# Transposing normalised activations with the DMA crossbar instead of TensorE, PSUM and ScalarE, in a four-layer kernel on one core

## The chip, the cores and the metric

The kernel runs on one core of a Trainium2 chip. The metric is the device time of one execution in microseconds (us), as the median over runs; one execution of each kernel was also profiled. A ratio is the mean time of one kernel's fast runs over the mean of the other's in the same rounds, so it is not quite the ratio of the medians quoted beside it.

## The reference, cut to what matters

One sequence of 2048 tokens with 576 features passes through four residual layers: attention-like, gated MLP, attention-like, gated MLP. The same weights serve both pairs.

```python
x = x + _A_ref(_layernorm(x), A_wqkv, A_w_phi, A_wo)     # "A": linear attention, 32 heads of 18
x = x + _B_ref(_layernorm(x), B_w_gate, B_w_up, B_w_down) # "B": (g * u) @ w_down, inner width 4608
x = x + _A_ref(_layernorm(x), ...)
x = x + _B_ref(_layernorm(x), ...)
```

Every layer needs the normalised x with features on the partitions (`xT`), while the normalisation itself works with tokens on the partitions. So each of the 16 tiles of 128 tokens is transposed once per layer, 64 times in all. Layer A first sums over all tokens; only after this barrier can its output be computed. A "pass" below is the part of layer A from its first projection to the barrier.

Of the kernel before, what the change touches and what calls it, by code (L numbers as in the profile page):

```python
# [6 lines left out]
BF16 = mybir.dt.bfloat16  # L7
F32 = mybir.dt.float32
ALU = mybir.AluOpType
# [423 lines left out]
def d_act(n, psum=False, ptrs=0):  # L433
    return n / 1.2 + (63.0 if psum else 92.0) + 93.0 * ptrs
# [10 lines left out]
class K:  # L445
    def __init__(self, nc, A_x, A_wqkv, A_w_phi, A_wo, B_w_gate, B_w_up, B_w_down, out, nlayers=4, dump=None):
        self.nc = nc
        self.A_x, self.A_wqkv, self.A_w_phi, self.A_wo = A_x, A_wqkv, A_w_phi, A_wo
        self.wg, self.wu, self.wd, self.out = B_w_gate, B_w_up, B_w_down, out
        self.nlayers = nlayers  # L450
        self.dump = dump
        self.nln0 = 3
        self.early = 2
        self.NPS, self.NSM, self.NVX, self.NET, self.NXP, self.NWD = 2, 4, 2, 3, 3, 3
        self.sbuf_check = True
        self.lag = 2
        self.bias = {10: 300.0}
        self.qfuse_after = ("ain", 1, 1)
        self.rawq_early = False
        self.v_early = False  # L460
        self.tr = Tracker()
        self.sc = Sched(self.tr)
        self.stack = ExitStack()

    def alloc(self):
        nc = self.nc
        A = lambda name, shape, dt: self.stack.enter_context(nc.sbuf_tensor(name, shape, dt))
        self.ident = A("ident", [128, 128], BF16)
        self.onesf = A("onesf", [128, 128], F32)
        self.epst = A("epst", [128, 1], F32)  # L470
        self.mask = A("mask", [TW, TW], BF16)
        self.ind = A("ind", [TW, HT], BF16)
        self.BDphi = A("BDphi", [TW, NT, TW], BF16)
        self.BD = A("BD", [TW, 2 * NT, 114], BF16)
        self.x_sb = A("x_sb", [128, NS, D], BF16)
        self.xT = A("xT", [128, 6, S], BF16)
        self.Wq = A("Wq", [128, 4, D], BF16)
        self.Wqr = A("Wqr", [128, 288], BF16)
        self.Wk = A("Wk", [128, 4, D], BF16)
        self.Wkr = A("Wkr", [128, 288], BF16)  # L480
        self.Wv = A("Wv", [128, 4, DP], BF16)
        self.Wvr = A("Wvr", [128, 324], BF16)
        self.Wo = A("Wo", [128, 4, D], BF16)
        self.Wor = A("Wor", [128, 288], BF16)
        self.Wg = A("Wg", [128, 4, FF], BF16)
        self.Wu = A("Wu", [128, 4, FF], BF16)
        self.Wr = A("Wr", [128, FF], BF16)
        AT = lambda name, shape, dt, base: nc.alloc_sbuf_tensor_at(name, shape, dt, offset=base)
        self.NG, self.NH = 3, 4
        al32 = lambda n: (n + 31) // 32 * 32  # L490
        raw_b = al32(5 * (2 * D + 72) * 2)
        wt_b = 2 * NT * 128 * 2
        wd_b = al32(self.NWD * CH * D * 2)
        ring_b = (self.NG + self.NH) * 256 * 2
        n1 = max(raw_b + wt_b, wd_b + ring_b)
        arena1 = A("arena1", [128, n1 // 2], BF16)
        a1 = nc.lookup_mloc(arena1).addr
        self.Wraw = AT("Wraw", [128, 5, 2 * D + 72], BF16, a1)
        self.WT = AT("WT", [TW, 2, NT, 128], BF16, a1 + raw_b)
        self.wdr = AT("wdr", [128, self.NWD, CH, D], BF16, a1)  # L500
        self.gsb = AT("gsb", [128, self.NG, 256], BF16, a1 + wd_b)
        self.hT = AT("hT", [128, self.NH, 256], BF16, a1 + wd_b + self.NG * 512)
        self.xln = A("xln", [128, 2 * self.NXP, 640], BF16)
        self.st = A("st", [128, 2 * self.NXP, 12], F32)
        self.mv = A("mv", [128, 2 * self.NXP, 2], F32)
        self.lnv = A("lnv", [128, 2 * self.NXP], F32)
        self.rstd = A("rstd", [128, 2 * self.NXP], F32)
        self.nmean = A("nmean", [128, 2 * self.NXP], F32)
        self.psb = A("psb", [128, self.NPS, D], BF16)
        self.mxmn = A("mxmn", [128, self.NPS, 2, H], F32)  # L510
        self.dd = A("dd", [128, self.NSM, 2, DP], BF16)
        self.ss = A("ss", [128, self.NSM, 2 * H], F32)
        self.rr = A("rr", [128, self.NSM, 2 * H], F32)
        self.wst = A("wst", [TW, NT, DH], BF16)
        self.vx = A("vx", [128, self.NVX, NT, TW + 1], BF16)
        self.eT = A("eT", [TW, self.NET, 2 * NT, 128], BF16)
        self.den = A("den", [128, self.NET, NT * HT], F32)
        self.rden = A("rden", [128, self.NET, NT * HT], F32)
        self.o = A("o", [128, self.NET, DP], BF16)
        self.oT = A("oT", [128, self.NET, 6, 128], BF16)  # L520
        self.ps = self.stack.enter_context(nc.psum_tensor("ps", [128, 8, 512], F32))
        self.psb16 = [self.ps[:, i, :].bitcast(BF16) for i in range(8)]
        self.sbuf_left = nc.sbuf_bytes_remaining
        sc = self.sc
        sc.pool("xlnp", self.NXP)
        sc.pool("sm", self.NSM)
        sc.pool("psb", self.NPS)
        self.vx_of = {}
        self.wt_of = {}
        sc.pool("vx", self.NVX)  # L530
        sc.pool("et", self.NET)
        sc.pool("wt", 2)
        sc.pool("wd", self.NWD)
        sc.pool("pb", 3)
        sc.pool("pbx", 2)
        self.banks = {"pb": [5, 6, 7], "pbx": [3, 4]}
        self.KV_BANKS = [0, 1, 2]
        self.GU_BANKS = [0, 1]
        self.ACC0 = 2
        self.wd_slot = {}  # L540
        self.g_wd = [self.tr.dma_group("wd%d" % i) for i in range(self.NWD)]
# [10 lines left out]
    def t_init(self):  # L552
        s = self
        yield ("ops", "dve", [
            Op(100, lambda e: e.memset(s.epst[:], EPS), writes=[("epst",)]),
            Op(100, lambda e: e.memset(s.wst[:, NT - 1, :], 0.0), writes=[("wst",)]),
            Op(300, lambda e: e.memset(s.xln[:, :, 576:640], 0.0), writes=[("xlnpad",)]),
        ])
        yield ("sig", "wstz")
        yield ("ops", "pool", [  # L560
# [5 lines left out]
               reads=[("onesf",)], writes=[("ident",)]),  # L566
# [3 lines left out]
               reads=[("onesf",)], writes=[("mask", 0)]),  # L570
# [3 lines left out]
               reads=[("onesf",)], writes=[("ind", 0)]),  # L574
# [5 lines left out]
               reads=[("mask", 0)], writes=[("mask", 0), ("mask",)]),  # L580
# [3 lines left out]
               reads=[("ind", 0)], writes=[("ind", 0), ("ind",)]),  # L584
# [3 lines left out]
        yield ("ops", "act", [  # L588
            Op(1000, lambda e: e.memzero(s.Wraw[64:128, 4, 0:2 * D]), writes=[("Wraw", 1)]),
            Op(300, lambda e: e.memzero(s.Wraw[:, :, 2 * D:2 * D + 72]), writes=[("Wraw", 2)]),  # L590
            Op(1800, lambda e: e.memzero(s.xT[0:64, 5, :]), writes=[("xTz",)]),
            Op(300, lambda e: e.memzero(s.Wv[:, :, D:DP]), writes=[("Wvpad",)]),
            Op(100, lambda e: e.memzero(s.Wvr[64:128, 252:324]), writes=[("Wvrpad",)]),
            Op(300, lambda e: e.memzero(s.oT[0:64, :, 5, :]), writes=[("oTz",)]),
# [147 lines left out]
    def t_ln(self, b, sig):  # L742
        s = self
        x_sb, xln, st, mv, lnv, rstd, xT = s.x_sb, s.xln, s.st, s.mv, s.lnv, s.rstd, s.xT
# [3 lines left out]
        ops = []  # L748
# [22 lines left out]
        for j in range(2):  # L771
            ops.append(Op(800, (lambda e, j=j: e.tensor_scalar(  # L772
                xln[:, sl[j], 0:576], x_sb[:, ss[j], :], nm[:, sl[j]:sl[j] + 1], rstd[:, sl[j]:sl[j] + 1],
                ALU.add, ALU.mult)),
                reads=[("x", ss[j], 0), ("x", ss[j], 1), ("nmean", pair), ("rstd", pair), ("xlnpad",)], writes=[("xln", sl[j])]))
        yield ("ops", "pool", ops)
        for j in range(2):
            got = yield ("acq", ["pb", "pbx"])
            bank = s.bank_of(got)
            pT = s.psb16[bank]  # L780
            ops = []
            for k in range(5):
                ops.append(Op(60, (lambda e, j=j, k=k, pT=pT: e.transpose(pT[:, 128 * k:128 * k + 128], xln[:, sl[j], 128 * k:128 * k + 128], s.ident[:])),  # L783
                              reads=[("xln", sl[j]), ("ident",)], writes=[("pbd", bank)], excl=[("pb", bank)]))
            yield ("ops", "pe", ops)
            tok = slice(128 * ss[j], 128 * ss[j] + 128)
            yield ("ops", "act", [
                Op(d_act(640, True), (lambda e, pT=pT, tok=tok: e.copy(xT[:, 0:5, tok], pT[:, 0:640].rearrange("p (k n) -> p k n", k=5))),
                   reads=[("pbd", bank)], writes=[("xT", ss[j], 0)], excl=[("pb", bank)]),
                Op(258, (lambda e, pT=pT, tok=tok: e.copy(xT[64:128, 5, tok], pT[0:64, 512:640])),  # L790
                   reads=[("pbd", bank), ("xTz",)], writes=[("xT", ss[j], 1)], excl=[("pb", bank)]),
            ])
            yield ("rel", got[0], got[1])
        yield ("rel", "xlnp", pair)
        yield ("sig", sig)

# [469 lines left out]
```

## The kernel before: what the change and the argument touch

The kernel writes one fixed instruction list per engine. Python generators describe the work of a tile, a list scheduler with its own time estimates decides in which order the pieces go onto each engine, and a tracker adds the semaphore waits. What matters here is that **every engine runs its list in order**, SyncE too, which issues all DMAs.

```python
self.nln0 = 3                 # pairs of tiles whose normalisation is launched at the start
self.NXP = 3                  # (in one line with others) buffers for a pair of normalised tiles
self.qfuse_after = ("ain", 1, 1)   # after which tile the q weights are prepared
```

The end of the normalisation of a pair of tiles:

```python
# GpSimd: xln = (x - mean) * rstd, 128 x 576
for j in range(2):
    got = yield ("acq", ["pb", "pbx"]); ...                     # a PSUM bank
    for k in range(5):                                          # TensorE, five 128x128 transposes
        Op(60, e.transpose(pT[:, 128*k:128*k+128], xln[:, sl[j], 128*k:128*k+128], s.ident[:]))
    Op(..., e.copy(xT[:, 0:5, tok], pT[:, 0:640]...))           # ScalarE, PSUM -> SBUF
    Op(258, e.copy(xT[64:128, 5, tok], pT[0:64, 512:640]))      # ScalarE, last 64 features once more
```

The loads, all on SyncE's queue, none of them waiting for anything:

```python
yield from xload(0); ...  # x, w_phi, k weights, v weights, rest of x, q weights, output weights
...
yield from grp("wgu", items, "wloaded")     # the MLP's gate and up weights, 10.6 MB, ten DMAs
```

The down weights are streamed in each MLP stage through three buffers (`wdr`), a chunk of 432 KB for three steps of the loop.

## Time and profile before

| | before |
|---|---|
| median | 1252.32 us (1251.99 to 1252.72) |
| first projection of the first pass | 19.7 us |
| first barrier | 97.5 us |
| first MLP stage | 125.1 to 641.2 us |
| second barrier | 703.2 us |
| second MLP stage | 732.2 to 1247.7 us |

The times of the stages are read from the start of the first projection, of the first barrier product and of the first gate matmul, and from the end of the last residual addition of each MLP stage. In the MLP stages TensorE is full; in the first pass VectorE is the fullest engine (71 of 77.5 us), with TensorE, ScalarE and GpSimd close behind (65 to 66 us). The lines for this stand in the prediction.

### The profile page before, as it was taken

The numbers are of one execution on the slowest core, as the hardware profiler recorded it, in microseconds if no ns is written. First come the engines' busy times: TensorE is split into PE (matmuls) and PEld (weight loads), VectorE is DVE, ScalarE is ACT, GpSimd is POOL, SyncE is SP. The second block draws the span as 40 slices with busy tenths as digits, with TensorE's granted clock in tenths as the row PEclk, the third lists the DMA queues.
The fourth block names the chain that finished last, engine by engine and source line by source line (L and its number), as shares of the span: only waits on it lengthen the run. The fifth ranks groups of instructions, "written<-read, shape, count | busy, mean of one in ns | idle before, by whom it ended". The sixth has DMA issues, their size and how long they took to land.

```text
span 1250.4 us, 25739 instructions
## 1 busy us (share of the span) xinstructions
PE 1198.8 (96%) x11096; PEld 936.1 (75%) x11096; DVE 619.3 (50%) x1478; ACT 546.4 (44%) x1393; POOL 272.5 (22%) x268
## 2 busy tenths in 40 slices
PE   6796999999999999999999889999999999999998
PEld 4574777778787777777767568778777777777776
DVE  6898646445553323323269974455445332323232
ACT  7887545445353323222258765444444322222222
POOL 4796212112120000000039742112112000000000
PEclk9998999999999999999999889999999999999999
DMA  9700122222222333333320002222222233323232
GB/s 316 230 2 1 41 75 72 74 85 72 85 73 86 88 99 89 98 90 97 94 64 2 1 2 73 86 82 74 82 84 82 86 97 99 105 91 110 87 109 67
DMA packets 85832, 104.61 MB, mean 84 GB/s; under 512 B 4374, under 2 KB 84566, under 8 KB 84566
## 3 DMA queue, kind: packets, MB, share of 16 engines
q1 hardware_dynamic: 85718, 102.96, 27.0%
q8 instruction: 87, 1.43, 0.5%
q14 instruction: 27, 0.22, 0.1%
HBM read 100.59 MB, written 2.36 MB: 82 GB/s over the span
## 4 chain that ended last, share of the span: by engine, by line
PE 84%; DVE 6%; POOL 5%; ACT 4%; issue 0%; DMA 0%; SPq 0%; DVEq 0%
PE ps L1071 25%; PE ps L1076 25%; PE ps L1109 20%; PE ps L808 4%; PE ps L1019 3%; POOL dd L869 3%; PE ps L1112 3%; DVE ss L855 2%; PE ps L946 2%; POOL dd L833 1%; PE ps L965 1%; PE ps L783 1%; DVE dd L841 1%; PE ps L998 1%; DVE mxmn L823 1%; DVE mxmn L828 1%
## 5 line engine op out<-in xcount | busy, mean ns | idle before, releaser
L1086 DVE TENSOR_TENSOR hT<-ps,gsb 128x256 bf16<-128x256 f32 x576 | 243.9, 423 | 577.2 <-ACT gsb L1084 575.9
L1084 ACT CAST gsb<-ps 128x256 bf16<-128x256 f32 x576 | 214.2, 372 | 621.7 <-PE ps L1076 585.3
L1109 PE MATMUL ps<-wdr,hT 128*128 128x512 bf16 x1152 | 357.5, 379 | 0.4 <-DVE x_sb L1135 0.4
L1071 PE MATMUL ps<-xT,Wg 128*128 128x256 bf16 x2304 | 347.2, 273 | 0.0
L1076 PE MATMUL ps<-xT,Wu 128*128 128x256 bf16 x2304 | 346.1, 273 | 0.0
L1071 PEld LDWEIGHTS ps<-xT,Wg 128*128 128x128 bf16 x2304 | 187.2, 98 | 80.8
L1076 PEld LDWEIGHTS ps<-xT,Wu 128*128 128x128 bf16 x2304 | 225.7, 98 | 26.4
L1112 PE MATMUL ps<-wdr,hT 128*128 128x64 bf16 x1152 | 221.9, 193 | 0.5 <-DVE x_sb L1138 0.5
L869 POOL TENSOR_TENSOR dd<-dd,rr 128x576 bf16<-128x576 bf16 x128 | 146.1, 1163 | 121.1 <-ACT rr L863 121.1
L1109 PEld LDWEIGHTS ps<-wdr,hT 128*128 128x128 bf16 x1152 | 112.6, 98 | 76.8 <-DVE x_sb L1135 0.7
L1071 PE MATMUL ps<-xT,Wr 128*128 128x256 bf16 x576 | 157.2, 273 | 0.0
L1076 PE MATMUL ps<-xT,Wr 128*128 128x256 bf16 x576 | 157.2, 273 | 0.0
L772 POOL TENSOR_SCALAR xln<-x_sb,nmean,rstd 128x576 bf16<-128x576 bf16 x64 | 51.9, 821 | 367.1 <-ACT rstd L767 366.9
L833 POOL TENSOR_TENSOR dd<-psb,mxmn 128x576 bf16<-128x576 bf16 x64 | 74.4, 1163 | 231.6 <-DVE mxmn L823 231.6
L1112 PEld LDWEIGHTS ps<-wdr,hT 128*128 128x128 bf16 x1152 | 112.7, 98 | 6.5 <-DVE x_sb L1138 0.8
L855 DVE TENSOR_REDUCE ss<-dd 128x64 f32<-128x1152 bf16 x64 | 86.4, 1350 | 22.8 <-ACT dd L850 22.5
L1071 PEld LDWEIGHTS ps<-xT,Wr 128*128 128x128 bf16 x576 | 56.5, 98 | 6.6
L1076 PEld LDWEIGHTS ps<-xT,Wr 128*128 128x128 bf16 x576 | 56.4, 98 | 6.6
L820 ACT CAST psb<-ps 128x288 bf16<-128x288 f32 x128 | 47.9, 400 | 17.3 <-PE ps L808 15.3
L949 ACT COPY eT<-ps 108x768 bf16<-108x768 bf16 x64 | 50.8, 798 | 8.5 <-PE ps L965 4.9
L828 DVE TENSOR_REDUCE mxmn<-ps 128x16 f32<-128x288 f32 x128 | 52.0, 448 | 0.0
L841 DVE TENSOR_TENSOR dd<-ps,mxmn 128x288 bf16<-128x288 f32 x128 | 51.7, 447 | 0.0
(85 smaller groups left out, 1143.8 us busy)
## 6 DMA issues: line engine op xcount, KB each, us to landing
wdr<-in_B_w_down_dram SPq DMA_DIRECT2D x192, 432.0 KB, 3.3
Wg<-in_B_w_gate_dram SPq DMA_DIRECT2D x4, 1152.0 KB, 12.3
Wu<-in_B_w_up_dram SPq DMA_DIRECT2D x4, 1152.0 KB, 27.3
x_sb<-in_A_x_dram SPq DMA_DIRECT2D x4, 576.0 KB, 5.8
out_dram<-x_sb SPq DMA_DIRECT2D x8, 288.0 KB, 3.7
Wraw<-in_A_wqkv_dram SPq DMA_DIRECT2D x8, 144.0 KB, 4.8
Wv<-in_A_wqkv_dram SPq DMA_DIRECT2D x1, 576.0 KB, 3.9
Wo<-in_A_wo_dram SPq DMA_DIRECT2D x1, 576.0 KB, 6.6
```

The lines of the kernel that those rows point to most:

```text
L772: ops.append(Op(800, (lambda e, j=j: e.tensor_scalar(xln[:, sl[j], 0:576], x_sb[:, ss[j], :], nm[:, sl[j]:sl[j] + 1], rstd[:, sl[j]:sl[j] ...
L828: ops.append(Op(370, (lambda e, h=h, pv=pv: e.tensor_reduce(mxmn[:, pz, 1, 16 * h:16 * h + 16], pv, AX.X, ALU.min)), reads=[("pbd", bank)] ...
L833: yield ("ops", "pool", [Op(1170, (lambda e: e.tensor_tensor(d1, p3, mxb, ALU.subtract)), reads=[("psb", pz, 0), ("psb", pz, 1), ("mx", pz ...
L841: ops.append(Op(370, (lambda e, d2h=d2h, pv=pv, mnbh=mnbh: e.tensor_tensor(d2h, pv, mnbh, ALU.subtract)), reads=[("pbd", bank), ("mn", pz, ...
L855: Op(1320, (lambda e: e.tensor_reduce(ss[:, sm, :].rearrange("p (b g) -> p b g", b=2), e4, AX.X, ALU.add)), reads=s.ddk(sm, 0) + s.ddk(sm, ...
L869: yield ("ops", "pool", [Op(1150, (lambda e, ev=ev, rb=rb: e.tensor_tensor(ev, ev, rb, ALU.mult)), reads=s.ddk(sm, br) + [("rr", sm), ("dd ...
L1071: ops.append(Op(d_pe(256), (lambda e, lhsT=lhsT, rhs=rhs, k=k, gub=gub: e.matmul(ps[:, gub, 0:256], lhsT, rhs, start=(k == 0), stop=(k == ...
L1076: ops.append(Op(d_pe(256), (lambda e, lhsT=lhsT, rhs=rhs, k=k, gub=gub: e.matmul(ps[:, gub, 256:512], lhsT, rhs, start=(k == 0), stop=(k = ...
L1084: yield ("ops", "act", [Op(372, (lambda e, g=g, gub=gub: e.copy(gsb[:, g, :], ps[:, gub, 0:256])), reads=[("GUg", gub)], writes=[("gsb", g ...
L1086: yield ("ops", "dve", [Op(425, (lambda e, g=g, h=h, gub=gub: e.tensor_tensor(hT[:, h, :], ps[:, gub, 256:512], gsb[:, g, :], ALU.mult)), ...
L1109: ops.append(Op(d_pe(512), (lambda e, lhsT=lhsT, bank=bank, slot=slot, fi=fi, f2=f2: e.matmul(ps[:, bank, 0:512], lhsT, s.wdr[:, slot, fi, ...
L1112: ops.append(Op(d_pe(64) + 6, (lambda e, lhsT=lhsT, sl=sl, slot=slot, fi=fi, f2=f2: e.matmul(ps[:, Z, 64 * sl:64 * sl + 64], lhsT, s.wdr[: ...
```

## The change

The intent is to take work from TensorE, which is full for most of the program, and from ScalarE and PSUM. The crossbar transpose is a DMA from SBUF to SBUF. It needs a 128 x 768 source with the last 64 features twice, so GpSimd writes a second small piece; the wider buffers leave room for two pairs only.

```diff
-        self.nln0 = 3
+        self.nln0 = 2
-        ... self.NXP, self.NWD = 2, 4, 2, 3, 3, 3
+        ... self.NXP, self.NWD = 2, 4, 2, 3, 2, 3
+        self.g_xt = [self.tr.dma_group("xt%d" % i) for i in range(2 * self.NXP)]
-        self.xln = A("xln", [128, 2 * self.NXP, 640], BF16)
+        self.xln = A("xln", [128, 2 * self.NXP, 768], BF16)
-            Op(1800, lambda e: e.memzero(s.xT[0:64, 5, :]), writes=[("xTz",)]),
+            ops.append(Op(200, (lambda e, j=j: e.tensor_scalar(
+                xln[:, sl[j], 704:768], x_sb[:, ss[j], 512:576], ...     # GpSimd, 128x64
-            (acquire a bank, five e.transpose on TensorE, two e.copy on ScalarE, release)
+            yield ("dma", s.g_xt[sl[j]], (lambda e, j=j, tok=tok: e.dma_start_transpose(xT[:, :, tok], xln[:, sl[j], :])), ...)
```

More of the change, by code (lines that the diff above doesn't have):

```diff
@@ L451, in __init__ @@
         self.dump = dump
-        self.nln0 = 3
+        self.nln0 = 2
         self.early = 2
-        self.NPS, self.NSM, self.NVX, self.NET, self.NXP, self.NWD = 2, 4, 2, 3, 3, 3
+        self.NPS, self.NSM, self.NVX, self.NET, self.NXP, self.NWD = 2, 4, 2, 3, 2, 3
         self.sbuf_check = True
@@ L556, in t_init @@
             Op(100, lambda e: e.memset(s.wst[:, NT - 1, :], 0.0), writes=[("wst",)]),
-            Op(300, lambda e: e.memset(s.xln[:, :, 576:640], 0.0), writes=[("xlnpad",)]),
+            Op(300, lambda e: e.memset(s.xln[:, :, 576:704], 0.0), writes=[("xlnpad",)]),
         ])
@@ L775, in t_ln @@
                 reads=[("x", ss[j], 0), ("x", ss[j], 1), ("nmean", pair), ("rstd", pair), ("xlnpad",)], writes=[("xln", sl[j])]))
+            ops.append(Op(200, (lambda e, j=j: e.tensor_scalar(
+                xln[:, sl[j], 704:768], x_sb[:, ss[j], 512:576], nm[:, sl[j]:sl[j] + 1], rstd[:, sl[j]:sl[j] + 1],
+                ALU.add, ALU.mult)),
+                reads=[("x", ss[j], 0), ("x", ss[j], 1), ("nmean", pair), ("rstd", pair), ("xlnpad",)], writes=[("xln", sl[j], 1)]))
         yield ("ops", "pool", ops)
         for j in range(2):
-            got = yield ("acq", ["pb", "pbx"])
-            bank = s.bank_of(got)
-            pT = s.psb16[bank]
-            ops = []
-            for k in range(5):
-                ops.append(Op(60, (lambda e, j=j, k=k, pT=pT: e.transpose(pT[:, 128 * k:128 * k + 128], xln[:, sl[j], 128 * k:128 * k + 128], s.ident[:])),
-                              reads=[("xln", sl[j]), ("ident",)], writes=[("pbd", bank)], excl=[("pb", bank)]))
-            yield ("ops", "pe", ops)
-            tok = slice(128 * ss[j], 128 * ss[j] + 128)
-            yield ("ops", "act", [
-                Op(d_act(640, True), (lambda e, pT=pT, tok=tok: e.copy(xT[:, 0:5, tok], pT[:, 0:640].rearrange("p (k n) -> p k n", k=5))),
-                   reads=[("pbd", bank)], writes=[("xT", ss[j], 0)], excl=[("pb", bank)]),
-                Op(258, (lambda e, pT=pT, tok=tok: e.copy(xT[64:128, 5, tok], pT[0:64, 512:640])),
-                   reads=[("pbd", bank), ("xTz",)], writes=[("xT", ss[j], 1)], excl=[("pb", bank)]),
-            ])
-            yield ("rel", got[0], got[1])
+            tok = slice(128 * ss[j], 128 * ss[j] + 128)
+            yield ("dma", s.g_xt[sl[j]], (lambda e, j=j, tok=tok: e.dma_start_transpose(xT[:, :, tok], xln[:, sl[j], :])),
+                   [("xln", sl[j]), ("xln", sl[j], 1)], [("xT", ss[j], 0), ("xT", ss[j], 1)], 128 * 768 * 2, False, True)
         yield ("rel", "xlnp", pair)
```

## The prediction

> **What bounds the kernel now.** I read the slice table first, to see where one engine is full and where none is.
>
> ```profile
> PE   6796999999999999999999889999999999999998
> DVE  6898646445553323323269974455445332323232
> POOL 4796212112120000000039742112112000000000
> DMA  9700122222222333333320002222222233323232
> ```
>
> Each digit is 31 us. There are four stages, two of each kind. In slices 0 to 3 and 20 to 23 (the attention-like halves) TensorE is not full and VectorE or GpSimd is. In slices 4 to 19 and 24 to 39 (the gated MLP halves, with the tail of the attention output mixed in) TensorE is full and little else matters. The DMA engines are full only in slices 0 and 1, when all weights are loaded.
>
> Second, the stretch table, which puts microseconds to this. Columns: busy time (count) of PE, weight load, VectorE, ScalarE, GpSimd, then granted clock, DMA share, GB/s.
>
> ```profile
> 20.00:97.50 77.50, 66.18 (x647) 48.72 (x646) 71.10 (x143) 66.37 (x179) 64.59 (x60) 1.00 0.44 152
> 125.00:160.00 35.00, 33.41 (x337) 26.77 (x336) 22.93 (x56) 20.81 (x50) 11.47 (x11) 0.99 0.13 40
> 160.00:400.00 240.00, 240.00 (x2299) 191.45 (x2298) 120.43 (x310) 108.31 (x274) 42.09 (x42) 1.00 0.26 78
> 400.00:640.00 240.00, 240.00 (x2145) 186.86 (x2143) 75.64 (x191) 64.37 (x178) 6.49 (x8) 1.00 0.32 94
> 747.00:1000.00 253.00, 251.81 (x2410) 200.47 (x2408) 125.46 (x317) 112.47 (x279) 44.65 (x43) 1.00 0.27 80
> ```
>
> From 20 to 97.5 us VectorE is busy 71.1 of 77.5 us: the first attention pass is VectorE-bound and can hardly be squeezed. From 160 to 640 us TensorE is busy in every microsecond, so each TensorE instruction taken out there shortens the program by its own length.
>
> Third, the same stretches for the TensorE transposes alone (PE, weight load, clock, DMA).
>
> ```profile
> 20.00:97.50 77.50, 4.12 (x50) 3.17 (x50) 1.00 0.44 152
> 125.00:160.00 35.00, 0.89 (x10) 0.73 (x10) 0.99 0.13 40
> 160.00:400.00 240.00, 7.99 (x90) 6.38 (x90) 1.00 0.26 78
> 400.00:640.00 240.00, 3.54 (x40) 2.91 (x40) 1.00 0.32 94
> 747.00:1000.00 253.00, 6.19 (x70) 5.09 (x70) 1.00 0.27 80
> ```
>
> Fourth, the start, in the timeline: when the first transposes and projections run, and what the SyncE queue is issuing then.
>
> ```profile
> 10.12 0.71 PE L783 MATMUL ps<-ident,xln 128*128 128x128 bf16 x5 [1.27 <-POOL xln L772]
> ...
> 15.00 2.21 SPq L670 DMA_DIRECT2D Wg<-in_B_w_gate_dram  x4
> ...
> 18.40 2.02 SPq L674 DMA_DIRECT2D Wu<-in_B_w_up_dram  x4
> ...
> 19.76 0.70 PE L808 MATMUL ps<-Wk,xT 128*128 128x288 bf16 x4
> ```
>
> The first token tile is transposed at 10.1 us and the first projection starts at 19.8 us, while SyncE is queueing the MLP weights up to 20.4 us. Those weights arrive much later; the view of the tile Wu and the page's list of DMA issues show it:
>
> ```profile
> DMA to landing us min/median/max: 23.8/27.3/30.8
> ```
>
> ```profile
> Wg<-in_B_w_gate_dram SPq DMA_DIRECT2D x4, 1152.0 KB, 12.3
> Wu<-in_B_w_up_dram SPq DMA_DIRECT2D x4, 1152.0 KB, 27.3
> ```
>
> The last Wu piece is issued at about 20.0 us and lands 30.8 us later, at 50.8 us. Today nothing on the early path waits for it.
>
> **What the Trainium skill says.** (1) "DMA: Bandwidth & Descriptors", section "Queues, rings and completion order": a queue has one ring on each DMA engine, and descriptors on an engine are consumed in ring order. The trace agrees: on the one queue the landing time grows in issue order, 12.3 us for Wg, 27.3 us for Wu. (2) The same page, "Latency and other measured facts", gives the DMA transpose 261 GB/s in one kernel; "Advanced Engine Details and Errata", section "X-Bar Transpose (TRN2)", says 350 to 400 GB/s. No run here shows it yet. (3) "VectorE: DVE Perf Modes", section "The three transpose paths": a 128x128 bf16 transpose is 390 ns on TensorE and 1309 ns by the crossbar. The trace has 219 ns for one on TensorE, and because they are pipelined, 0.089 us each in the stream (7.99 us / 90).
>
> **The change part by part.**
>
> Removed from TensorE: 64 token tiles x 5 = 320 transposes. Only those in TensorE-bound stretches count: 0.89 + 7.99 + 3.54 = 12.4 us in 125 to 640 us, and 6.2 us in 747 to 1000 us. Sum 18.6 us gained. The 4.1 us in the first pass lie beside a full VectorE and count little.
>
> Removed from ScalarE: 64 evictions of 128x640 (692 ns) and 64 of 64x128 (257 ns), together 61 us, and one clearing of xT (1.04 us). ScalarE bounds no long stage; I count 2 to 3 us in the first pass, where it is 86% busy beside VectorE, and nothing elsewhere.
>
> Added to GpSimd: 64 copies of 128x64. The 128x576 one costs 821 ns; in proportion the small one is 91 ns, and with some fixed cost I estimate 0.2 us. Sixteen of them are in the first pass: 3 us on an engine busy 64.6 of 77.5 us. I count 1 us.
>
> Added to the DMA: 64 transposes of 128 x 768 x 2 B = 196,608 B. The wdr loads (442,368 B) land 3.3 us after issue; at the 330 GB/s that the weight load reaches in 20 to 40 us, 1.3 us of this is data, so about 2 us is fixed. With 261 GB/s for the transpose (0.75 us) I estimate 2.7 us, say 3 us, from issue to landing. The unfavourable reading, six 128-column blocks at 1.31 us one after another, is 7.9 us; I give that little weight, since it counts the fixed part six times.
>
> Moved: the transposes now go through SyncE, an in-order engine with one queue. The scheduler gives every weight load to SyncE before the first transpose, because the loads wait for nothing. **This is the main term.** The first transposes can be issued after 20.4 us at the earliest, and in ring order they stand behind all the MLP weights. They move when those have landed, at 50.8 us; the first xT tile is there at about 52 us and the first projection starts at about 52.5 instead of 19.8 us: 32.7 us late. What can be done in the hole? Little: the q weights are fused only after a processed tile, and with two xln pairs only the statistics of four pairs of tiles run ahead, which they did before too. From there the first pass needs its VectorE time of 71 us plus a few us to start, 75 instead of 77.8 us. So the barrier comes at about 127.5 instead of 97.5 us: +30 us.
>
> Start of each MLP stage: before, the second xln tile of the first pair is ready at 122.3 us and the gate matmuls start 3.1 us later (125.4). Now two small GpSimd copies (0.4 us) and a transpose of some 3 us stand there. About +1 us each, +2 us for both. Later pairs have a whole block (36 steps of 1.58 us, 57 us) of slack. Pairs for the second attention pass are normalised one MLP block at a time and are hidden as well; only the last pair, ready at 647 us, could matter, and there TensorE no longer stands waiting for xln (3.7 us of waits). I count 0.
>
> Weight stream of the MLP: one wdr chunk is used in 3 x 1.58 = 4.7 us, three buffers, so a load has 9.5 us less 3.3 us of landing: about 6 us of slack. A pair of transposes ahead of it on the queue costs about that, or less if they overlap. I count +2 us in all.
>
> Sum: 1252.3 + 30 + 1 + 2 + 2 - 18.6 = 1268.7; the ScalarE relief is already inside the 75 us. I round to 1268 us.
>
> **The rivals.**
>
> A: the transposes do not wait behind the weights. Then the 30 us are gone and the change is 18.6 us gained less some 5 us: about 1239 us, within 2%. Against it: the rising landing times. For it: no trace here has a crossbar transpose, and it might be served apart. I give it 1 in 9.
>
> B: the transpose is slow, 5 to 8 us, and does not overlap with its neighbour. Then in the first pass sixteen of them need 80 to 128 us against VectorE's 71 us, and the barrier comes up to 50 us later still; and a pair would take 10 to 16 us of the wdr loads' 6 us of slack, so TensorE would stall in many blocks. That makes 1290 to 1400 us. For it: 1309 ns for one 128x128 block. Against it: both bandwidth figures. I give it 1 in 5.
>
> C: the TensorE gain is not collected, because SyncE stands in order, with a transpose waiting for xln holding up a wdr load that is ready. Its time would be about 1280 us. Against it: the three buffers, and that the scheduler places both by their ready times.
>
> D: the gain is all there is and the late start is absorbed by the stages after. Against it: the barrier needs all sixteen tiles, and TensorE is full from 160 us on, so nothing later can absorb it.
>
> **Range and chances.** The main case spreads by the late start (27 to 34 us) and the MLP hiccups (0 to 10 us): 1260 to 1280. Rival A pulls the lower end down, B the upper end up: 1245 to 1295. Faster by 2% needs less than 1227.8 us, more than even A gives: 0.02. Slower by 2% needs over 1277.3 us: B, C and the upper edge of the main case: 0.30. The rest, 0.68.
>
> **What would show each step.** The late start: the first projection at 50 to 55 us and TensorE nearly idle between 22 and 50 us; if it is at 25 us, rival A. The transposes' size: landing 2.5 to 4 us after issue in quiet stages, 25 us or more for the first four. The TensorE gain: PE busy time down by about 24 us in all and each MLP stage shorter by 12 and 6 us from its first to its last matmul. Rival B or C: waits of TensorE for wdr in the MLP stages, which are absent today. A landing time near 8 us, or a barrier much later than 130 us, would make the prediction wrong on the slow side.

## The result

The changed kernel takes 1280.68 us (median of 4 runs, 1279.59 to 1282.26) against 1252.15 us; the ratio is 1.0229, interval 1.0214 to 1.0243. It is slower by just over 2%, and correct.

By stage, from both traces (us):

| stage | before | after | difference |
|---|---|---|---|
| start to first projection | 19.7 | 52.0 | +32.3 |
| first pass, to the barrier | 77.8 | 86.5 | +8.7 |
| barrier to first gate matmul | 27.6 | 28.1 | +0.5 |
| first MLP stage | 516.1 | 510.9 | -5.2 |
| second pass, to its barrier | 62.0 | 61.9 | -0.1 |
| barrier to gate matmul | 29.0 | 28.5 | -0.5 |
| second MLP stage | 515.5 | 506.9 | -8.6 |
| sum | 1247.7 | 1274.8 | +27.1 |

All of the loss is before the first barrier (41.0 us); the stages after it give 13.9 us back. The slice table of the changed kernel's page shows the hole:

```profile
PE   1388689999999999999999969999999999999998
DVE  3297865554645333232328986555554332323232
POOL 2287641221311000000006963222121000000000
DMA  9812013333323343443321002333233433333332
```

In the first two slices (64 us) TensorE, VectorE and GpSimd are busy for only one to three tenths of the time, while the DMA engines are full. The SyncE rows of the changed kernel's timeline from 13 to 60 us, and the TensorE rows from 50 to 58 us, say what was awaited:

```profile
18.16 2.01 SPq L674 DMA_DIRECT2D Wu<-in_B_w_up_dram  x4
20.21 39.17 SPq L783 DMA_TRANSPOSE xT<-xln  x8
```

```profile
51.97 1.14 PE L799 MATMUL ps<-Wk,xT 128*128 128x288 bf16 x4 [38.76 <-DMA xT<-xln]
...
56.86 0.65 PE L799 MATMUL ps<-Wk,xT 128*128 128x288 bf16 x4
```

The first transpose is issued right behind the last weight load, and the 38.76 us for which TensorE sat idle before its first projection end when it lands. The two rows also show that the first matmuls after the hole run at about half pace: four take 1.14 us at 52 us and 0.65 us at 57 us.

The view of the transposing line, the page's list of DMA issues, and the view of the added GpSimd line (nanoseconds: minimum, median, maximum):

```profile
DMA to landing us min/median/max: 2.5/2.6/31.7
```

```profile
xT<-xln SPq DMA_TRANSPOSE x64, 2.6
```

```profile
L776 POOL TENSOR_SCALAR xln<-x_sb,nmean,rstd x64: 390/393/398, 10.0 to 1003.6; 128x64 bf16<-128x64 bf16 x64
```

A transpose of 196,608 B lands in 2.6 us where nothing stands in its way. The small GpSimd copy takes 0.39 us, half as long as one of nine times the width.

The stretches of the changed kernel that answer to those of before, with the same columns:

```profile
52.00:138.50 86.50, 67.57 (x591) 47.58 (x592) 70.98 (x142) 56.89 (x153) 69.83 (x74) 0.95 0.22 48
200.00:440.00 240.00, 236.83 (x2206) 189.47 (x2244) 124.12 (x317) 96.32 (x246) 52.17 (x63) 1.00 0.34 94
440.00:677.00 237.00, 235.06 (x2060) 184.03 (x2095) 75.94 (x192) 57.35 (x162) 9.45 (x16) 1.00 0.37 97
```

In the first pass no engine is busy for more than 71 of 86.5 us, where before VectorE was busy for 71 of 77.8 us. In the MLP stages TensorE seems to have small gaps, but this trace lacks 162 of the 1152 matmuls of one line (990 are recorded), so I do not read them as idle time; the lengths of the blocks, below, are the sounder measure.

### The profile page after: what moved, and what is told of

Same layout as the page of the kernel before. It is cut to its first block, busy times and chain, and to the rows that moved or that the text cites. A ratio compares the mean times of both kernels' runs of the same rounds, so it can differ in the third digit from the quotient of the medians.

```text
span 1277.9 us, 24939 instructions
## 1 busy us (share of the span) xinstructions
PE 1172.5 (92%) x10614; PEld 919.1 (72%) x10776; DVE 618.4 (48%) x1478; ACT 490.1 (38%) x1264; POOL 295.7 (23%) x332
## 4 chain that ended last, share of the span: by engine, by line
PE 82%; POOL 7%; DVE 3%; DMA 3%; ACT 2%; SPq 1%; issue 1%; DVEq 0%
PE ps L1062 25%; PE ps L1067 24%; PE ps L1100 17%; PE ps L1103 5%; PE ps L799 5%; POOL dd L860 4%; PE ps L1010 3%; DMA xT<-xln 3%; POOL dd L824 2%; PE ps L937 2%; PE ps L956 1%; DVE ss L846 1%; PE ps L989 1%; POOL xln L772 1%; ACT eT L940 0%
## 5 line engine op out<-in xcount | busy, mean ns | idle before, releaser
L1100 PE MATMUL ps<-wdr,hT 128*128 128x512 bf16 x990 | 318.1, 380 | 0.4 <-DVE x_sb L1126 0.4
L772 POOL TENSOR_SCALAR xln<-x_sb,nmean,rstd 128x576 bf16<-128x576 bf16 x64 | 52.5, 820 | 403.2 <-ACT rstd L767 365.1
L799 PE MATMUL ps<-Wk,xT 128*128 128x288 bf16 x256 | 41.9, 291 | 42.0 <-DMA xT<-xln 38.8
L814 DVE TENSOR_REDUCE mxmn<-psb 128x32 f32<-128x576 bf16 x64 | 47.7, 746 | 44.1 <-ACT psb L811 44.0
L799 PEld LDWEIGHTS ps<-Wk,xT 128*128 128x128 bf16 x256 | 24.7, 99 | 50.9 <-DMA xT<-xln 38.9
```

Of the source, the lines that this page charges most:

```text
L772: ops.append(Op(800, (lambda e, j=j: e.tensor_scalar(xln[:, sl[j], 0:576], x_sb[:, ss[j], :], nm[:, sl[j]:sl[j] + 1], rstd[:, sl[j]:sl[j] ...
L799: ops.append(Op(d_pe(ncol), (lambda e, lhsT=lhsT, rhs=rhs, k=k: e.matmul(s.ps[:, bank, 0:ncol], lhsT, rhs, start=(k == 0), stop=(k == 4))) ...
L1100: ops.append(Op(d_pe(512), (lambda e, lhsT=lhsT, bank=bank, slot=slot, fi=fi, f2=f2: e.matmul(ps[:, bank, 0:512], lhsT, s.wdr[:, slot, fi, ...
```

## The experiments

Three questions were open: is it the order in the queue that makes the start late; why is the first pass 8.7 us longer; and what did the MLP stages gain per transpose, with what hidden costs. All kernels gave correct results.

### weights_act: the MLP weights on another queue

```diff
+        yield ("wait", ("xT", 1, 1))                     # after the first two pairs are normalised
-        yield from grp("wgu", items, "wloaded")
+        yield from grp("wgu", items, "wloaded", "act")   # ScalarE issues these ten DMAs
```

(Here and in own_ring the scheduler keeps a DMA estimate for each queue, so it also lays out another order of instructions.)

> The changed kernel, but the ten MLP weight loads are issued from ScalarE's DMA queue, after the first two pairs of tiles are normalised; the transposes stay on SyncE's queue. Theory (the transposes wait behind the weights because they share a ring): the first transposes land within some 3 to 8 us of their issue, the first projection starts at 20 to 26 us instead of 52 us, and the time falls by about 28 us to 1250 to 1256 us. Rival (it is the load on the DMA engines, or the crossbar is held up by any large load, whatever the queue): the first projection stays at about 50 us and the time at about 1280 us.

Measured: 1286.7 us, ratio 1.0282 (1.0226 to 1.0338), and the first projection at 59.3 us, later than in the changed kernel. So moving the weights away from the transposes' ring did not help at all. The test was not clean: the q weights and the output weights still stood before the transposes on SyncE's queue, and the output weights landed 28.5 us after issue (37.3 us for their small remainder, in two pieces) instead of 6.7 us. The next run cleans this.

### own_ring: nothing before the transposes on their queue

```diff
-        (q weights and output weights on SyncE's queue before the MLP weights)
+        (output weights, MLP weights, q weights, in this order, all on ScalarE's queue)
```

> The changed kernel, but ScalarE's DMA queue issues the MLP weights, the output projection's weights and the q weights, in this order; so on SyncE's queue nothing but the finished early loads stands before the first transposes, and both queues are active from about 12 us. Ring order as the cause: the first transposes land within 15 us of their issue, first projection before 30 us. Rival (two rings share the engines unfairly, or a crossbar transpose is held up by loads on the engines whatever the ring): first projection at 45 us or later, as in the run with only the MLP weights moved (59 us), where two small loads still stood before the transposes.

Measured: 1297.49 us (two runs, 1291.7 and 1303.28; the time itself is of little use, since the q weights now come last). First projection at 25.5 us. But it is one tile only; the TensorE rows of this kernel's timeline, 24 to 30 and 40 to 50 us:

```profile
25.46 1.14 PE L801 MATMUL ps<-Wk,xT 128*128 128x288 bf16 x4 [12.48 <-DMA xT<-xln]
```

```profile
44.40 1.14 PE L801 MATMUL ps<-Wk,xT 128*128 128x288 bf16 x4 [16.20 <-DMA xT<-xln]
```

and the landing times of the first 150 us, followed by the stretch from 20 to 50 us in this kernel and in the changed one (columns as before; the last is GB/s):

```profile
DMA to landing us min/median/max: 2.5/3.2/53.6
```

```profile
20.00:50.00 30.00, 6.51 (x25) 3.43 (x25) 0.00 (x0) 0.00 (x0) 0.00 (x0) 0.53 1.05 243
20.00:50.00 30.00, 0.00 (x0) 0.00 (x0) 0.00 (x0) 0.00 (x0) 0.00 (x0) 0.50 1.02 345
```

The first two transposes, issued at 10.7 and 12.5 us, land at 25.4 and 44.4 us, while the last MLP weights land at 70 us. This alone proves little, since both were issued before the first MLP weight load (13.5 us). The trace's records of single DMA packets decide it. In the changed kernel no 256 B piece of a transpose starts before 49.1 us, when the weights run out (their last piece starts at 50.4 us), so on the shared queue **ring order is the cause**. With a ring of their own the transposes move all the time, but slowly. The counts from 30 to 60 us in own_ring (q1 is SyncE's queue, q10 ScalarE's; packets, MB, share of the engines):

```profile
q10 hardware_dynamic: 1071, 7.38, 94.3%
q1 hardware_dynamic: 1074, 0.27, 8.5%
```

The two queues take turns packet by packet, and not byte by byte: 1074 packets of some 250 B against 1071 of some 6.9 KB. A transpose consists of 800 packets (the changed page counts 51,200 more for 64 transposes), so about as many weight packets pass beside it. My estimate from these numbers, 800 x 7.1 KB at 256 GB/s, is 22 us for each transpose; the first three land 19 and 25 us apart (25.4, 44.4 and 69.5 us), and one took 53.6 us from issue to landing. So the rival was right too: beside a full load a crossbar transpose is slow even with a ring to itself. Either of the two is enough to make the first pass late. The load is slowed as well: from 20 to 50 us the DMA engines move 243 GB/s, against 345 GB/s in the changed kernel, where almost only weights move. Why the total falls I did not settle.

### weights_late: the MLP weights after the first pass's transposes

```diff
+        yield ("wait", ("xT", 1, NB - 1))
         yield from grp("wgu", items, "wloaded")
```

> The changed kernel, but the MLP weight loads are given to SyncE only after the transposes of the first pass; nothing large is then on the DMA engines while these move. Both theories of the late start (ring order, busy engines) expect the same: first projection at 20 to 25 us, the transposes landing in 2.6 to 4 us. The pass stays long (84 to 88 us, two pairs), the barrier comes at about 107 us, and the time is 1280.7 - 30 = 1250 us, 1246 to 1256. If the weights arrive too late for the MLP, the first gate matmul is later than 137 us.

Measured: 1251.06 us, ratio 0.9983 (0.9964 to 1.0002). First projection at 22.8 us, the pass 87.2 us, barrier at 110.0 us, gate matmul at 138.1 us; the weights, issued from 72 us, were in time. Taking the load out of the way in time gives back 29.6 us (1280.68 - 1251.06). The late start is thereby confirmed as the main loss, and the remaining 9 us of the pass as a separate one.

### two_pairs: the buffers alone

```diff
 (the kernel before)
-        self.nln0 = 3
+        self.nln0 = 2
-        ... self.NXP, self.NWD = 2, 4, 2, 3, 3, 3
+        ... self.NXP, self.NWD = 2, 4, 2, 3, 2, 3
```

> The kernel before with two xln pairs and two pairs launched ahead, as the change needs for its room; the transposes stay on TensorE. It prices the buffers alone. Theory (the longer first pass of the changed kernel, 86.5 against 77.8 us, and of the first-pass-on-TensorE run, 88.0 us, comes from having two pairs, which gives another instruction order): pass 86 to 89 us and 1260 to 1264 us. Rival (it comes from the GpSimd copies or the crossbar): pass about 78 us and 1252 us.

Measured: 1260.49 us, ratio 1.0064 (1.0043 to 1.0086), pass 88.4 us. With all transposes on TensorE and no small copies, two pairs alone make the pass 10.6 us longer. Of this 8 us reach the end.

### late_pe: the late start alone

```diff
 (the kernel before: the first pass's TensorE transposes also wait for the MLP weights)
-                              reads=[("xln", sl[j]), ("ident",)], ...
+                              reads=[("xln", sl[j]), ("ident",)] + ([("Wu",)] if sig[:2] == ("xT", 1) else []), ...
```

> The kernel before, but the TensorE transposes of the first pass wait for the MLP weights (one more dependence). No crossbar transpose, no GpSimd copy, three pairs. This is the late start alone. Theory: first projection at about 52 us, the pass then takes 75 to 78 us as before, barrier at about 130 us, time 1282 to 1286 us. Rival (a late start itself makes the pass longer, because less can run ahead): pass about 86 us as in the changed kernel, barrier at about 138 us, time 1291 us or more.

Measured: 1294.25 us, ratio 1.0331 (1.0315 to 1.0347); first projection at 52.9 us, pass 89.0 us. My theory fell here: with three pairs, the pass after a late start is long as well. So two pairs are enough to lengthen the pass, and a late start is enough too, and in the changed kernel, which has both, they do not add. What they have in common is that each makes the scheduler lay out another instruction order: in the traces VectorE's sequence departs from that of the kernel before after 21 instructions in late_pe and after 29 in two_pairs.

### after_order: another order, nothing else

```diff
 (the changed kernel)
-        self.qfuse_after = ("ain", 1, 1)
+        self.qfuse_after = ("ain", 1, 5)
```

> The changed kernel with one number changed: the q weights are fused after token tile 5 of the first pass instead of tile 1. Same work, same buffers, same late start; only the static order of instructions is another. Theory (the pass of 86.5 us instead of 78 us is a worse instruction order, not an engine at its limit): the kernel's own plan says a barrier 8 us earlier and 8 us less in all: pass 78 to 80 us, 1272 to 1276 us. Rival (GpSimd, with its extra copies, or the crossbar limits the pass): pass 85 us or more, about 1280 us.

Measured: 1269.14 us, ratio to before 1.0146 (1.0123 to 1.0169), so 11.5 us less than the changed kernel. First projection at 51.2 us, pass 76.5 us. The pass in three kernels, as stretches of before, of two_pairs and of after_order:

```profile
19.70:97.50 77.80, 66.48 (x650) 48.98 (x648) 71.40 (x143) 66.64 (x180) 64.59 (x60) 1.00 0.44 153
```

```profile
18.60:107.00 88.40, 70.30 (x662) 50.71 (x663) 74.73 (x149) 70.30 (x186) 67.10 (x63) 0.99 0.42 140
```

```profile
51.20:127.70 76.50, 65.34 (x594) 47.00 (x595) 70.74 (x143) 57.96 (x153) 70.72 (x74) 0.97 0.26 55
```

VectorE (third pair) and GpSimd (fifth) do as much in 76.5 us here as in the changed kernel in 86.5 us: 70.74 against 70.98 us and 70.72 against 69.83 us. What the order changes is how long the engines wait for each other. The waits of GpSimd and VectorE for ScalarE in the pass of the changed kernel, and then of after_order (us in total, times, longest):

```profile
POOL dd L860 <- ACT rr L854: 12.3, 8, 3.1
DVE ss L846 <- ACT dd L841: 10.9, 6, 2.6
```

```profile
POOL dd L860 <- ACT rr L854: 1.6, 2, 1.4
DVE ss L846 <- ACT dd L841: 0.2, 1, 0.2
```

Neither GpSimd with its copies nor the crossbar set the length of the pass; the order did, and with two pairs and a late start both in place. One number that adds and removes no work is worth 11.5 us.

### pe_first and pe_first_n3: the first pass on TensorE, the rest by crossbar

pe_first takes the changed kernel and brings back, for the first pass alone, the TensorE and ScalarE lines shown under "the kernel before", and leaves out the small GpSimd copy there. pe_first_n3 also has three pairs again:

```diff
-        self.nln0 = 2
+        self.nln0 = 3
-        ... self.NXP, self.NWD = 2, 4, 2, 3, 2, 3
+        ... self.NXP, self.NWD = 2, 4, 2, 3, 3, 3
-        self.den, self.rden, self.onesf: own tensors
+        (den and rden over the tail of the weight arena, free after the q weights; onesf over eT)
```

> The changed kernel, but the first attention pass transposes on TensorE as before (without the extra GpSimd copy there); the other 48 token tiles go through the crossbar. Two xln pairs, as in the changed kernel. Theory (all of the loss is in the first pass, and the later stages gained 5.0 + 0.9 + 8.3 us): first projection at about 20 us, barrier at 97 to 102 us, time 1236 to 1243 us, which beats both kernels. Rival (the crossbar also costs in the later stages, hidden by something else): 1250 us or more.

> First pass on TensorE, the rest by crossbar, and three xln pairs again; the room is found by laying den and rden over a finished part of the weight arena and an initialisation constant over eT. Theory (two pairs cost 9 to 10 us in the pass, and the later stages gain 14 to 18 us): pass 78 us, time 1252.5 - 15 = 1237 us, 1233 to 1241, faster than both kernels. Rival (the pairs do not matter): about 1246 us, as with two pairs.

Measured: pe_first 1246.48 us, ratio 0.9945 (0.9924 to 0.9966), slower than I expected because its pass takes 88.0 us: this is what led to two_pairs. pe_first_n3 takes 1239.0 us, ratio 0.9888 (0.9871 to 0.9905), with a pass of 78.8 us. It is faster than both kernels, by 1.1% against the kernel before. Its MLP stages take 508.7 and 506.9 us, 7.4 and 8.6 us less than before.

### late_n3_order: the crossbar in every pass, repaired

This is weights_late with three pairs as in pe_first_n3 and the q weights prepared after tile 9.

> All three repairs with the crossbar in every pass: MLP weights given to SyncE after the first pass's transposes, three pairs, q weights fused after tile 9. First projection at about 22.5 us, pass 75 to 79 us, later stages as in the changed kernel: 1239 to 1245 us, faster than the kernel before by about 1%. If it is at or below 1239 us, the crossbar is worth having in the first pass too; if above, TensorE is the better place there.

Measured: 1241.75 us (1235.72 to 1245.14), ratio 0.9914 (0.9882 to 0.9946), pass 78.4 us. Also faster than before, but its interval overlaps that of pe_first_n3, so which place is better for the first pass stays open.

### twice_pe: the price of a TensorE transpose

```diff
 (the kernel before)
-            for k in range(5):
+            for k in (range(5) if sig[:2] == ("xT", 1) else [0, 0, 1, 1, 2, 2, 3, 3, 4, 4]):
```

> The kernel before, but outside the first pass every TensorE transpose is done twice (240 more). It prices a transpose in the full TensorE stream. Prediction's figure, 0.089 us each from the busy column: 46 tiles x 5 x 0.089 = 20 us more, 1272 us. Rival, 0.055 us each from the block lengths (57.5 against 56.9 us for 10 transposes): 12.7 us more, 1265 us.

Measured: 1264.01 us, ratio 1.0092 (1.0076 to 1.0107), 11.2 us over its own reference of 1252.8. (The diff doubles the transposes of 48 tiles; the 46 in the expectation was a slip.) The two MLP stages together are 11.3 us longer and hold 210 of the added transposes, but the sum hides an uneven split: the first stage takes 10.7 us more (516.1 to 526.8) for 140 added transposes, the second only 0.6 us (515.5 to 516.1) for 70. The early blocks of each stage, which have attention output mixed in, change by some us with the order. The clean measure is a quiet block. These are the last residual additions of two successive blocks of the first MLP stage, from the timelines of before, of the changed kernel and of twice_pe:

```profile
528.56 0.21 DVE L1138 TENSOR_TENSOR x_sb<-ps,x_sb 128x64 bf16<-128x64 f32 x1
...
586.06 0.21 DVE L1138 TENSOR_TENSOR x_sb<-ps,x_sb 128x64 bf16<-128x64 f32 x1
```

```profile
565.96 0.21 DVE L1129 TENSOR_TENSOR x_sb<-ps,x_sb 128x64 bf16<-128x64 f32 x1
...
622.90 0.21 DVE L1129 TENSOR_TENSOR x_sb<-ps,x_sb 128x64 bf16<-128x64 f32 x1
```

```profile
538.83 0.21 DVE L1138 TENSOR_TENSOR x_sb<-ps,x_sb 128x64 bf16<-128x64 f32 x1
...
596.89 0.21 DVE L1138 TENSOR_TENSOR x_sb<-ps,x_sb 128x64 bf16<-128x64 f32 x1
```

57.50 us with 10 transposes, 56.94 without, 58.06 with 20: 0.056 us each way. In the trace of before, the five transposes of a group start 0.056 us apart and the next matmul starts 0.056 us after the last of them, while that one, 0.219 us long, is still running.

### twice_dma: the price of a crossbar transpose in the MLP stages

```diff
 (pe_first_n3)
+            for _ in range(2):
                 yield ("dma", s.g_xt[sl[j]], (lambda e, ...: e.dma_start_transpose(xT[:, :, tok], xln[:, sl[j], :])), ...)
```

> The best kernel so far (first pass on TensorE, three pairs) with every crossbar transpose issued twice, 48 more of 196,608 B. If the crossbar transposes are hidden in the later stages: 1239 us plus 1 to 4 us (2.6 us more ahead of the first gate matmul of each MLP stage, nothing elsewhere). Rival (they hold up the weight stream of the MLP, six us of slack): 8 us more or worse, 1247 us or more, and TensorE waits for wdr.

Measured: 1237.08 us, ratio 0.9883 (0.9868 to 0.9897), no slower than pe_first_n3. From the barriers to the gate matmuls it loses (29.4 to 33.8 us, 26.9 to 33.7 us), and the MLP stages then get shorter by about as much (508.7 to 503.2, 506.9 to 501.5). I suppose that other work fills the wait and is then out of the way; no run shows this by itself. The only TensorE wait on the crossbar after 150 us in the view of waits (us in total, times, longest):

```profile
PE ps L1086 <- DMA xT<-xln: 0.3, 1, 0.3
```

No wait for wdr is listed. In the later stages the crossbar transposes cost nothing in the sum, even when there are twice as many.

## Why the prediction was right or wrong

The time lay in the stated range, 12.7 us above the figure, and on the side that I had given 0.30: slower by over 2%. The main term held; two others were mis-sized, and neither error was foreseen. That the time is still inside the range is partly luck: it lies just above the main case's own 1260 to 1280 us, and the range went up to 1295 us for slow transposes (rival B), which did not come; what filled that room was a longer first pass.

**The late start: right in size and in direction.** The prediction had the first projection at 52.5 us; it is at 52.0. The reason given, ring order, is right for this kernel and incomplete: own_ring shows that on a ring of their own the transposes would still crawl, packet by packet, beside the load. Rival A, "served apart", is refuted for the changed kernel, and a second queue is no way out; what helped was a later load (weights_late, 29.6 us). One sign was wrong: the first four transposes were to land 25 us or more after issue, but only the first did (31.7 us, then 10.9, 5.0 and 2.7 us), because SyncE was held for 21.6 us on issuing it and issued the others late.

**The first pass of 75 us: the step that failed.** It was taken from VectorE's busy time, as if the order of the instructions would stay as good as before. Measured 86.5 us, 11.5 us more than the 75. The busy times were read correctly, and after_order shows a pass of 76.5 us with the same work and buffers. What the argument left out is that the instruction order is made by a scheduler from its own time estimates, so that it changes with the diff. The two settings for the pairs (tested together in two_pairs, where the pass is 10.6 us longer) and the late start (late_pe, 11.2 us) each lead to an order with longer waits. The settings looked like a detail of the diff.

**The TensorE gain of 18.6 us: mechanism right, size too large.** The MLP stages gained 5.2 + 8.6 = 13.8 us. The mis-sized term is "0.089 us each in the stream", and with it the sentence that a TensorE instruction taken out shortens the program by its own length: the figure divided a group's busy time by its count, but the tail of a group of five runs beside the next matmul. The marginal price is 0.056 us (the quiet blocks), which makes 210 x 0.056 = 11.8 us. The remaining 2.0 us of the measured gain I did not trace, and the split does not fit either: at this price the first stage should gain 7.8 us and the second 3.9, and not 5.2 and 8.6 (the prediction had 12 and 6). The quiet blocks agree in all kernels with the same transposes, so the difference lies in the early blocks, whose lengths vary by some us between kernels with the same transposes. The other sign, TensorE busy for 24 us less, can't be checked, as the changed kernel's trace lacks matmuls. The Trainium skill had the warning that I did not use: "Trainium Kernel Development and Optimization", section "Performance Expectations", calls matmul busy time a bad metric for how close a kernel is to its roofline (the hardware's limit), because matmuls are pipelined. These runs agree, for the price of a single instruction: 0.089 us by busy time, 0.056 us by the length of a block.

**The crossbar's own time: right.** Estimated 2.7 to 3 us, measured 2.6 us. Rival B, a slow transpose, is refuted for a quiet DMA; beside a full load, in own_ring, the transposes were far slower even than it said (19 and 25 us from one landing to the next).

**The small terms.** The GpSimd copy takes 0.39 us and not 0.2 us, 3 us more in a pass that GpSimd did not bound. The starts of the MLP stages cost 0 and not 2 us. The hiccups of the weight stream, 2 us, are 0: twice_dma shows no TensorE wait for it. Rival C has no support: the MLP stages became shorter. Rival D was rightly excluded, as the late start reaches the end almost whole.

In sum: 1268.7, plus 11.5 for the pass, plus 4.8 for the smaller TensorE gain, less about 5 for the small terms, is 1280, and 1280.7 was measured. The corrections are themselves taken from the measured stages, so this shows only that no large term is missing.

## What to carry to other kernels

Before you move a transfer onto a DMA queue, ask what stands on that queue, and on the engines, at the time of its first use: here a 2.6 us transpose became one of 31.7 us because 10.6 MB of weights that nobody needed for another 70 us had been issued first. Price an instruction in a full pipelined stream by the length of a stretch with and without it (or with it twice) or by the distance from start to start, not by its busy time. And where a scheduler lays out the instruction order, test the settings that a change drags along by themselves and try a few neighbouring orders before you judge the change: here the same idea was worth +2.3%, or -0.9% with three pairs, a better order and a later load (-1.1% with the first pass left on TensorE).

## What the Trainium skill lacked or had wrong

- "DMA: Bandwidth & Descriptors", section "Rules for kernel authors", says that a transpose next to ordinary DMAs needs nothing. All results here were correct, so as a rule of safety nothing here speaks against it; this rule says nothing of speed. Beside a full weight load from another queue a transpose took up to 53.6 us instead of 2.6 us, and from 20 to 50 us the engines moved 243 GB/s instead of 345.
- "VectorE: DVE Perf Modes", section "The three transpose paths": 1309 ns by the crossbar and 390 ns on TensorE for 128x128. Here six such blocks in one DMA land in 2.6 us, 0.43 us a block, and a TensorE transpose costs 0.056 us in a full stream (219 ns as a single instruction, without the copy out of PSUM). Neither single duration gives the price in this kernel.
- "DMA: Bandwidth & Descriptors", section "Latency and other measured facts", gives a bandwidth for the DMA transpose and no time from issue to landing: it is 2.6 us for 196,608 B, 76 GB/s if one divides.
- For the issue time of such a transpose I found no trn2 figure for this shape: the fastest took 1.21 us on SyncE, against 0.37 us for a plain load of 432 KB, and up to 21.6 us with the queue full of weights.
- In the pages that I read I found no fixed cost of a small GpSimd tensor_scalar: 128x64 takes 0.393 us and 128x576 0.820 us, so about 0.34 us of each is fixed.
